# Chaining the first projections' low parts with the norms' statistics on VectorE, and the second chunk's statistics ahead of the first projection, in a two-layer transformer kernel

## The chip, the core and the metric

The kernel runs on one core of a Trainium2 chip. The metric is the device time of one execution in microseconds; 3 runs of the kernel before are shown. Five engines have instruction streams of their own: TensorE (PE; its weight loads are PEld), VectorE (DVE), ScalarE (ACT), GpSimd (POOL) and SyncE (SP), which only issues DMAs here. ScalarE issues DMAs as well, in line with its arithmetic: a DMA that has to wait for its data holds up what stands behind it on ScalarE.

## The reference

Two layers of the same weights, each with an attention block and a dense block, on x of 2048 rows and 512 columns:

```python
def _A_ref(x, wqkv, wo):                      # 32 heads of 16
    qkv = (x @ wqkv).reshape(B, S, 3, H, Dh).transpose(2, 0, 3, 1, 4)
    q, k, v = qkv[0], qkv[1], qkv[2]
    p = softmax(einsum("bhqd,bhkd->bhqk", q, k) * (Dh ** -0.5))
    o = einsum("bhqk,bhkd->bhqd", p, v)
    return o.transpose(0, 2, 1, 3).reshape(B, S, D) @ wo
def _B_ref(x, w1, b1, w2):                    # 512 -> 1792 -> 512
    h = x @ w1 + b1
    return (h * tanh(log1p(exp(-|h|)) + max(h, 0))) @ w2
for _ in range(2):
    x = x + _A_ref(layernorm(x), A_wqkv, A_wo)
    x = x + _B_ref(layernorm(x), B_w1, B_b1, B_w2)
```

## The kernel before

**Numbers.** Every large product is made of three matmuls of fp32r parts. A value is split into a high part (ScalarE copies it, rounded) and a low part (VectorE subtracts the high part from it), and the product is the sum of high by high, low by high and high by low: `mm3` (L159 to L164), and `mm3_by_kind` (L152 to L157) for the first two projections. `split_psum` (L148) is that split for a result that lies in PSUM, the matmuls' accumulator memory.

**Tiling.** The 2048 rows are cut into four chunks of 512. A chunk is normalised in four tiles of 128 rows and transposed, so that its columns can be multiplied by the weights. The projections to q, k are units (m, c): m is 0 to 3 for q's and 4 to 7 for k's blocks of 128 columns, c is the chunk; such a unit is 12 matmuls into one PSUM bank of the "s" kind, of which there are three. Units of v have four tiles of 12 matmuls each. The order of the units of layer 0 is a list written by hand: six of chunk 0, four of chunk 1, (3, 0), then (0, 2), (4, 2), (7, 0), (2, 1), (6, 1), (0, 3), (4, 3) and the others.

**Layer 0's start.** `first_norm` (L685) normalises chunk 0 at once, with warm-up matmuls in between. Chunks 1 to 3 are normalised by `norm_parts` (L166), a generator of five steps: first the statistics of the four tiles (L177 and L178 on VectorE, four pairs, chained with one another), the variance (L173) on VectorE and its power on GpSimd (L174); then four times a normalised tile (L196 on VectorE, name xnq), four transposes on TensorE (L201, bank tpq of the "n" kind, two of them), and the split (high thq L149 on ScalarE, low tlq L150 on VectorE). `steps` (L770) puts these steps ahead of given places in the list of units: chunk 1's five at 1 to 5 of the numbers it is given, chunk 2's from 6, chunk 3's from 11.

**After a unit**, `evict` (L455) splits its bank into pt (one of three buffers, shared with the raw weights that are being split in `make`, L111) and ScalarE issues the store scr<-pt (L458). When m 0 and m 4 of three chunks are stored, `prep_qk` (L230) issues on SyncE the loads of the first heads' rows of q and k (qs, ks; L249), then those of the last chunk. `some_max` (L446) puts pairs of score matmuls (pm, pn; L273) between the last units, whose maxima VectorE takes (L291, L306). A v tile is copied by ScalarE into one half of vst (L504) and stored by SyncE (L505).

**What sets the order.** The helper `Order` (L83) ties each instruction handed to it to the last one handed to it on the same engine: a fixed order with no semaphore. `front` is such a chain, used by `first_norm`, the statistics in `norm_parts`, and the first two units' matmuls. The attention has a chain of its own, in which all of its matmuls, reductions and exponentials stand. Whatever is in no chain is placed by a planner, which models the engines' times when the program is built and orders each engine's instructions by that model.

The lines that the change touches:

```python
def split_psum(hi, lo, src):
    nc.scalar.activation(hi, src, AF.Copy)
    nc.vector.tensor_tensor(lo, src, hi.bitcast(F32), op=ALU.subtract)
...
for c, at in ((1, range(1, 7)), (2, range(6, 12)), (3, range(11, 17))):
    steps(before, at, norm_parts(xc[c], f"q0{c}", tt, c, "n", o=front))
```

## Time and profile before

| | |
|---|---|
| median of 3 runs | 3481.96 us (3481.78 to 3482.94) |
| the profiled execution | 3478.88 us |
| its span, first to last instruction | 3476.9 us |
| TensorE busy | 3444.9 us, 99% of the span |
| VectorE busy | 2971.3 us, 85% |
| ScalarE busy | 2622.1 us, 75% |
| mean granted clock of TensorE | 0.996 of full speed |

The program has four stages in each layer: projections (0 to some 186 us in layer 0), attention, the output projection, and the dense block. Layer 1 begins near 1743 us. A busy share is a mean over stages that are bound by different engines, so the rows below are read stage by stage. Matmuls are pipelined: a row's duration is longer than its distance to the next one, and it is the distance that counts in a full stretch.

### The profile page before, as it was taken

To read this page: it belongs to the slowest core of one execution; us is meant where nothing else is said; L and a number is where in the kernel's file an instruction comes from. 1 tells how busy PE (TensorE), PEld (TensorE's weight loads), DVE (VectorE), ACT (ScalarE), POOL (GpSimd) and SP (SyncE) were. 2 spreads that over 40 slices of the span, in tenths; PEclk is the share of its full clock that TensorE was granted. 3 is DMA by queue.
4 is the path that set the end of the run, shared out by engine and by line. 5 is a ranking of instruction groups with operands and counts; after the bars stand their busy time and mean duration, and the time that the engine had idled before them with its cause. 6 is when DMAs were issued, how large, how long until landed. Compare 5 with 4: busy or idle time off the path is not lost.

```text
span 3476.9 us, 71195 instructions
## 1 busy us (share of the span) xinstructions
PE 3444.9 (99%) x29075; PEld 1919.7 (55%) x29075; DVE 2971.3 (85%) x4155; ACT 2622.1 (75%) x4893; POOL 282.1 (8%) x329
## 2 busy tenths in 40 slices
PE   9999999999999999999999999999999999999999
PEld 6644444444444444888876444444444444448887
DVE  6699999999999996665537999999999999956554
ACT  3188899899989887356532889998988998964665
POOL 1000000000000001222200000000000000012222
PEclk9999999999999999999999999999999999999999
DMA  7641312213122114500264202112021220154000
GB/s 257 223 108 34 81 43 74 61 54 80 45 58 55 31 55 122 180 13 13 86 200 154 53 15 46 35 27 49 20 48 20 42 43 18 56 144 157 13 13 25
DMA packets 131863, 247.39 MB, mean 71 GB/s; under 512 B 30928, under 2 KB 72400, under 8 KB 116432
## 3 DMA queue, kind: packets, MB, share of 16 engines
q1 hardware_dynamic: 110960, 186.21, 21.3%
q10 hardware_dynamic: 20576, 56.63, 4.2%
q8 instruction: 229, 3.75, 0.5%
q14 instruction: 98, 0.80, 0.1%
HBM read 149.43 MB, written 92.27 MB: 70 GB/s over the span
## 4 chain that ended last, share of the span: by engine, by line
DVE 66%; PE 29%; DMA 2%; issue 1%; ACT 1%; SPq 0%; DVEq 0%; ACTq 0%
DVE mxv L306 33%; DVE mxv L291 32%; PE h L164 3%; PE h L163 3%; PE h L162 3%; PE mo L162 3%; PE mo L163 3%; PE mo L164 3%; PE qk L162 1%; PE qk L163 1%; PE qk L164 1%; PE sp L353 1%; PE pv L379 1%; PE va L162 1%; PE wo L162 1%
## 5 line engine op out<-in xcount | busy, mean ns | idle before, releaser
L355 ACT ACTIVATE p<-sp 128x512 f32<-128x512 f32 x4096 | 2134.6, 598 | 239.6 <-PE pn L273 142.6
L291 DVE TENSOR_REDUCE mxv<-pm 128x2 f32<-128x1024 f32 x1024 | 1239.6, 1211 | 80.7 <-PE pm L273 80.7
L306 DVE TENSOR_REDUCE mxv<-pn 128x1 f32<-128x512 f32 x2048 | 1304.1, 675 | 2.8 <-PE pn L273 2.6
L353 PE MATMUL sp<-qs,ks 50*128 50x512 f32 x4096 | 1290.2, 447 | 0.2
L379 PE MATMUL pv<-p,va 128*32 128x256 f32 x16384 | 1196.7, 388 | 1.9 <-DVE pt L150 1.9
L353 PEld LDWEIGHTS sp<-qs,ks 50*128 50x128 f32 x4096 | 569.9, 184 | 712.1 <-ACT p L355 627.5
L273 PE MATMUL pn<-ks,qs 48*128 48x512 f32 x2048 | 824.0, 449 | 1.2 <-DVE mxv L306 0.9
L379 PEld LDWEIGHTS pv<-p,va 128*32 128x32 f32 x16384 | 377.6, 108 | 547.2 <-issue 428.9
L273 PE MATMUL pm<-ks,qs 48*128 48x512 f32 x2048 | 436.3, 421 | 1.0 <-DMA ks<-scr 1.0
L273 PEld LDWEIGHTS pn<-ks,qs 48*128 48x128 f32 x2048 | 365.6, 183 | 8.3 <-DVE mxv L306 2.7
L273 PEld LDWEIGHTS pm<-ks,qs 48*128 48x128 f32 x2048 | 193.1, 185 | 64.1 <-issue 8.0
L318 POOL CAST nh<-nm 128x16 fp32r<-128x16 f32 x64 | 12.7, 198 | 2437.4 <-DVE nm L313 2437.4
L633 POOL TENSOR_TENSOR hb<-hb,he 128x512 f32<-128x512 f32 x112 | 148.5, 1326 | 474.4 <-DVE he L630 474.4
L162 PE MATMUL mo<-w,ah 128*128 128x512 f32 x448 | 176.0, 394 | 3.4 <-ACT ah L636 3.3
L163 PE MATMUL mo<-w,ah 128*128 128x512 f32 x448 | 175.4, 392 | 0.0
L164 PE MATMUL h<-thm,w 128*128 128x512 f32 x448 | 175.0, 391 | 0.0
L163 PE MATMUL h<-tlm,w 128*128 128x512 f32 x448 | 174.9, 390 | 0.0
L162 PE MATMUL h<-thm,w 128*128 128x512 f32 x448 | 174.7, 391 | 0.0
L164 PE MATMUL mo<-w,al 128*128 128x512 f32 x448 | 166.8, 392 | 0.0
L635 DVE TENSOR_TENSOR hb<-hb,hr 128x512 f32<-128x512 f32 x112 | 77.3, 690 | 98.9 <-ACT hr L632 73.1
L627 ACT ACTIVATE hb<-h,b1t 128x512 f32<-128x512 f32 x112 | 76.9, 687 | 97.7 <-PE h L164 77.2
L149 ACT ACTIVATE pt<-qk 128x512 fp32r<-128x512 f32 x64 | 38.0, 598 | 146.8 <-PE qk L164 119.4
(130 smaller groups left out, 2555.0 us busy)
## 6 DMA issues: line engine op xcount, KB each, us to landing
scr<-pt ACTq DMA_DIRECT2D x64, 512.0 KB
ks<-scr SPq DMA_DIRECT2D x168, 128.0 KB
qs<-scr SPq DMA_DIRECT2D x168, 128.0 KB
vscr<-vst SPq DMA_DIRECT2D x32, 512.0 KB
va<-vscr SPq DMA_DIRECT2D x16, 1024.0 KB
w<-w1p SPq DMA_DIRECT2D x14, 1024.0 KB
w<-w2p SPq DMA_DIRECT2D x14, 1024.0 KB
raw<-ot SPq DMA_DIRECT2D x256, 32.0 KB
```

Of the source, the lines that this page charges most:

```text
L162: pe(nc.tensor.matmul(acc, ah, bh, start=first and i == 0, stop=False))
L163: pe(nc.tensor.matmul(acc, ah, bl, start=False, stop=False))
L164: pe(nc.tensor.matmul(acc, al, bh, start=False, stop=last and i == n - 1))
L273: nc.tensor.matmul(out, qs[h // 2][rows, q0 : q0 + P], ks[h // 2][rows, ts(c, 512)], start=True, stop=True)
L291: self.order(nc.vector.tensor_reduce(self.mxs[b][:, 0:2, qt, c], pm, axis=AX.X, op=ALU.max))
L306: self.order(nc.vector.tensor_reduce(self.mxs[b][:, h, qt, c : c + 1], pm, axis=AX.X, op=ALU.max))
L353: nc.tensor.matmul(sp, ks[h // 2][rows, ts(kt, P)], qs[h // 2][rows, ts(qb, CW)], start=True, stop=True)
L355: return lambda: self.order(nc.scalar.activation(self.pts[s][:, h], sp, AF.Exp, scale=SCALE))
L379: nc.tensor.matmul(acc[ts(h, VW), cols], va[:, kt, h, :], self.pts[s][:, h, cols], start=kt == 0 and half == 0, stop=kt == NKT - 1, skip_g ...
L627: nc.scalar.activation(hb, acc, AF.Identity, bias=b1t[:, f : f + 1])
L633: nc.gpsimd.tensor_tensor(hb, hb, e, op=ALU.mult)
L635: nc.vector.tensor_tensor(hb, hb, r, op=ALU.mult)
```

## The change

`split_psum` and `evict` get an argument o through which the low part's instruction on VectorE is passed. In layer 0 (where `first` is the chain `front`) the first 12 units in the list pass `front`, so their low parts stand in one chain with the statistics of chunks 1 to 3, in the order in which the program is written. The five steps of chunk 1's norm, at places 1 to 5 before, are at 0, 2, 3, 4 and 5: the statistics are ahead of the first unit.

```diff
--- before.py
+++ after.py
@@ -145,9 +145,9 @@
         nc.sync.dma_start(t.bitcast(F32), wparts[kind, j])
         return t
 
-    def split_psum(hi, lo, src):
+    def split_psum(hi, lo, src, o=lambda ins: ins):
         nc.scalar.activation(hi, src, AF.Copy)
-        nc.vector.tensor_tensor(lo, src, hi.bitcast(F32), op=ALU.subtract)
+        o(nc.vector.tensor_tensor(lo, src, hi.bitcast(F32), op=ALU.subtract))
 
     def mm3_by_kind(acc, pairs, pe=lambda ins: ins):
         n = len(pairs)
@@ -452,9 +452,9 @@
                 att.max_one()
                 att.max_one()
 
-        def evict(m, c, acc):
+        def evict(m, c, acc, o=lambda ins: ins):
             pt = tmp.tile([P, 2, CW], F32R, tag="raw", name=f"pt{l}{m}{c}", bufs=3)
-            split_psum(pt[:, 0], pt[:, 1], acc)
+            split_psum(pt[:, 0], pt[:, 1], acc, o)
             nc.scalar.dma_start(
                 scr[m][:, :, ts(c, CW)].bitcast(F32).rearrange("a p n -> p a n"), pt.bitcast(F32)
             )
@@ -516,7 +516,7 @@
                     pe=first if first and i < 2 else pe,
                 )
                 left -= 1
-                evict(m, c, acc)
+                evict(m, c, acc, first if first and i < 12 else lambda ins: ins)
                 if m in (0, 4):
                     done += 1
                     if done >= 2 * NCH - 2 and done % 2 == 0:
@@ -767,7 +767,7 @@
         at(i, lambda j=j: load_qkv(0, wts, (j,), later=wait, stores=stores, lo="dve"))
     for n in range(6):
         at(19 + n, lambda n=n: stores[n]())
-    for c, at in ((1, range(1, 7)), (2, range(6, 12)), (3, range(11, 17))):
+    for c, at in ((1, (0, 2, 3, 4, 5, 6)), (2, range(6, 12)), (3, range(11, 17))):
         steps(before, at, norm_parts(xc[c], f"q0{c}", tt, c, "n", o=front))
     for l in range(2):
         if l == 0:
```

The planner's order follows. Names: qk, then layer, chunk and m (qk020 is chunk 2, m 0); pt, then layer, m and chunk (pt002 is the same unit's split result); tpq, xnq: layer, chunk, tile; thq, tlq, stq, mvq: layer, chunk; vm: split weights of v; scr: the store's target, by layer and m. The number behind _ is a buffer's.

VectorE, around chunk 2's statistics, before:

```order
L150 TENSOR_TENSOR tlq01_272<-tpq012_331,thq01_271 128x4x128
L150 TENSOR_TENSOR tlq01_272<-tpq013_361,thq01_271 128x4x128
L178 BN_AGGR mvq03_529<-stq03_528 128x2
L177 BN_STATS stq03_528<-x03_103 128x6
L196 TENSOR_SCALAR xnq020_421<-x02_101,mvq02_389,rsq02_391 128x512
L196 TENSOR_SCALAR xnq021_450<-x02_101,mvq02_389,rsq02_391 128x512
L178 BN_AGGR mvq03_529<-stq03_528 128x2
L177 BN_STATS stq03_528<-x03_103 128x6
L150 TENSOR_TENSOR pt060_381<-qk006_368,pt060_381 128x512
L178 BN_AGGR mvq03_529<-stq03_528 128x2
L173 TENSOR_SCALAR veq03_530<-mvq03_529 128x4
L150 TENSOR_TENSOR pt001_415<-qk010_402,pt001_415 128x512
```

The two first normalised tiles of chunk 2 stand here ahead of pt060 and pt001, chunk 2's statistics are above this piece, and chunk 3's are spread over it. VectorE at the same place after:

```order
L150 TENSOR_TENSOR tlq01_272<-tpq012_331,thq01_271 128x4x128
L150 TENSOR_TENSOR tlq01_272<-tpq013_361,thq01_271 128x4x128
L150 TENSOR_TENSOR pt060_381<-qk006_368,pt060_381 128x512
L177 BN_STATS stq02_388<-x02_101 128x6
L178 BN_AGGR mvq02_389<-stq02_388 128x2
L177 BN_STATS stq02_388<-x02_101 128x6
L178 BN_AGGR mvq02_389<-stq02_388 128x2
L177 BN_STATS stq02_388<-x02_101 128x6
L178 BN_AGGR mvq02_389<-stq02_388 128x2
L177 BN_STATS stq02_388<-x02_101 128x6
L178 BN_AGGR mvq02_389<-stq02_388 128x2
L150 TENSOR_TENSOR pt001_415<-qk010_402,pt001_415 128x512
```

Chunk 2's four pairs now stand together between pt060 and pt001, and no statistics of chunk 3 are here.

TensorE, ahead of the first matmuls of chunk 2 (- before, + now):

```order
 L163 MATMUL qk003_511<-tlq00_111,qkm1_192 128x512
 L164 MATMUL qk003_511<-thq00_110,qkm1_192 128x512
+L201 MATMUL tpq022_478<-ident_70,xnq022_476 128x128 x4
+L201 MATMUL tpq023_504<-ident_70,xnq023_502 128x128 x4
 L162 MATMUL qk020_542<-thq02_419,qkm0_91 128x512
 L162 MATMUL qk024_570<-thq02_419,qkm2_95 128x512
-L201 MATMUL tpq030_563<-ident_70,xnq030_561 128x128 x4
+L162 MATMUL qk007_628<-thq00_110,qkm3_196 128x512
+L163 MATMUL qk007_628<-tlq00_111,qkm3_196 128x512
```

The last two tiles' transposes now stand directly ahead of chunk 2's first matmul, which is followed by qk007, a unit of chunk 0, instead of a transpose of chunk 3.

ScalarE at the same place, before:

```order
L149 ACTIVATE pt051_498<-qk015_485 128x512
L149 ACTIVATE thq02_419<-tpq022_478 128x4x128
L149 ACTIVATE thq02_419<-tpq023_504 128x4x128
L458 DMA scr05_205<-pt051_498 128x2x512
L149 ACTIVATE pt030_524<-qk003_511 128x512
L149 ACTIVATE thq03_559<-tpq030_563 128x4x128
L458 DMA scr03_203<-pt030_524 128x2x512
L149 ACTIVATE pt002_555<-qk020_542 128x512
```

Chunk 2's last two high parts (thq02) stand one behind the other here, ahead of two stores. ScalarE at the same place after:

```order
L149 ACTIVATE pt051_498<-qk015_485 128x512
L149 ACTIVATE thq02_419<-tpq020_423 128x4x128
L121 ACTIVATE vm1_355<-vr1_356 128x512 x2
L458 DMA scr05_205<-pt051_498 128x2x512
L149 ACTIVATE thq02_419<-tpq021_452 128x4x128
L149 ACTIVATE pt030_524<-qk003_511 128x512
L149 ACTIVATE thq02_419<-tpq022_478 128x4x128
L458 DMA scr03_203<-pt030_524 128x2x512
L149 ACTIVATE thq02_419<-tpq023_504 128x4x128
L149 ACTIVATE pt002_555<-qk020_542 128x512
L458 DMA scr00_200<-pt002_555 128x2x512
```

Now each of the last three has an eviction (pt051, pt030) or a store's issue (L458) ahead of it.

VectorE at the start of layer 1, where the last chunk's sums of layer 0's dense block (x203, L655) and its statistics (L584 to L586) meet the first low parts of layer 1, before:

```order
L655 TENSOR_TENSOR x203_18378<-mo03_20684,x203_18378 128x512 x2
L584 BN_STATS stq13_21363<-x203_18378 128x6
L585 BN_AGGR mvq13_21364<-stq13_21363 128x2
L584 BN_STATS stq13_21363<-x203_18378 128x6 x2
L585 BN_AGGR mvq13_21364<-stq13_21363 128x2
L586 TENSOR_SCALAR veq13_21365<-mvq13_21364 128x1
L585 BN_AGGR mvq13_21364<-stq13_21363 128x2 x2
L586 TENSOR_SCALAR veq13_21365<-mvq13_21364 128x1 x3
L597 TENSOR_SCALAR xnq130_21485<-x203_18378,mvq13_21364,rsq13_21366 128x512
L597 TENSOR_SCALAR xnq131_21504<-x203_18378,mvq13_21364,rsq13_21366 128x512
L150 TENSOR_TENSOR pt102_21384<-qk120_21371,pt102_21384 128x512
```

The first low part of layer 1, pt102, closes this piece. VectorE at the same place after:

```order
L584 BN_STATS stq13_21363<-x203_18378 128x6 x2
L655 TENSOR_TENSOR x203_18378<-mo03_20684,x203_18378 128x512 x2
L585 BN_AGGR mvq13_21364<-stq13_21363 128x2 x2
L584 BN_STATS stq13_21363<-x203_18378 128x6 x2
L586 TENSOR_SCALAR veq13_21365<-mvq13_21364 128x1 x2
L585 BN_AGGR mvq13_21364<-stq13_21363 128x2
L150 TENSOR_TENSOR pt102_21384<-qk120_21371,pt102_21384 128x512
L150 TENSOR_TENSOR pt140_21405<-qk104_21392,pt140_21405 128x512
```

The low parts pt102 and pt140 move ahead of the normalised tiles xnq130 and xnq131. On TensorE the last dense tile's 12 matmuls (mo, L162 to L164) stand behind 20 matmuls of the units qk120, qk104 and qk114 there, and ahead of them before.

Other places move by some rows: stores of weights (L128, on ScalarE) by up to 8 rows at 16 places of the attention, the loads of the last chunk's qs on SyncE.

## Rows read from the trace of the kernel before

**Rows 1.** The page's first part: busy time, share of span, instructions.

```profile
PE 3444.9 (99%) x29075; PEld 1919.7 (55%) x29075; DVE 2971.3 (85%) x4155; ACT 2622.1 (75%) x4893; POOL 282.1 (8%) x329
```

**Rows 2.** Busy time by stretch: window, length, PE, PEld, DVE, ACT, POOL, PEclk, DMA share, GB/s.

```profile
40.00:60.00 20.00, 20.00 (x103) 16.71 (x102) 11.55 (x20) 8.47 (x16) 0.00 (x0) 1.00 0.48 181
60.00:80.00 20.00, 18.98 (x83) 14.74 (x82) 6.42 (x9) 3.88 (x7) 0.00 (x0) 1.00 1.00 271
80.00:100.00 20.00, 19.31 (x86) 14.99 (x84) 4.06 (x6) 2.83 (x5) 0.00 (x0) 1.00 0.96 370
100.00:120.00 20.00, 19.12 (x78) 13.15 (x80) 11.21 (x15) 4.20 (x8) 0.00 (x0) 0.91 0.94 310
...
220.00:300.00 80.00, 80.00 (x818) 36.22 (x820) 79.93 (x108) 72.24 (x140) 7.62 (x8) 1.00 0.26 61
```

**Rows 3.** TensorE's timeline: start, duration, line, operation, tile, [idle before <- what ended it].

```profile
33.18 0.73 PE L162 MATMUL qk<-thq,qkm 128*128 128x512 f32 x2 [1.09 <-ACT thq L149]
34.85 0.50 PE L163 MATMUL qk<-tlq,qkm 128*128 128x512 f32 x1 [0.93 <-DVE tlq L150]
...
49.96 0.62 PE L162 MATMUL qk<-thq,qkm 128*128 128x512 f32 x2
...
65.54 0.61 PE L162 MATMUL qk<-thq,qkm 128*128 128x512 f32 x2
67.17 0.47 PE L273 MATMUL pm<-ks,qs 48*128 48x512 f32 x1 [1.02 <-DMA ks<-scr]
...
75.95 0.50 PE L162 MATMUL qk<-thq,qkm 128*128 128x512 f32 x1
...
100.88 0.50 PE L162 MATMUL va<-vm,thq 128*128 128x512 f32 x1 [1.57 <-ACT vst L504]
```

**Rows 4.** Chain of waits from 0 to 200 us: start, share of time, what.

```profile
57.72 4.35 DMA scr<-pt
...
63.82 3.32 DMA ks<-scr
...
71.78 5.08 DMA scr<-pt
...
89.81 6.01 DMA scr<-pt
...
97.01 3.12 DMA vscr<-vst
100.23 0.61 ACT vst L504
...
101.61 0.23 PE va L164
...
102.87 0.43 PE va L162
```

**Rows 5.** VectorE's timeline in layer 0's start.

```profile
15.07 0.68 DVE L177 BATCH_NORM_STATS2 stq<-x 128x6 f32<-128x512 f32 x1
...
15.89 0.66 DVE L177 BATCH_NORM_STATS2 stq<-x 128x6 f32<-128x512 f32 x1
...
23.81 1.00 DVE L196 TENSOR_SCALAR xnq<-x,mvq,rsq 128x512 f32<-128x512 f32 x2
...
35.38 0.98 DVE L196 TENSOR_SCALAR xnq<-x,mvq,rsq 128x512 f32<-128x512 f32 x2
...
36.95 0.67 DVE L150 TENSOR_TENSOR pt<-qk,pt 128x512 fp32r<-128x512 f32 x1
...
38.31 0.69 DVE L150 TENSOR_TENSOR pt<-qk,pt 128x512 fp32r<-128x512 f32 x1 [0.40 <-ACT pt L149]
```

**Rows 6.** GpSimd's timeline in layer 0's start.

```profile
19.54 1.02 POOL L174 TENSOR_TENSOR rsq<-veq,mhalf 128x4 f32<-128x4 f32 x1 [9.44 <-DVE veq L173]
```

**Rows 7.** VectorE's timeline at the start of layer 1.

```profile
1756.29 1.29 DVE L655 TENSOR_TENSOR x<-mo,x 128x512 f32<-128x512 f32 x2 [0.30 <-PE mo L164]
...
1763.72 1.29 DVE L150 TENSOR_TENSOR pt<-qk,pt 128x512 fp32r<-128x512 f32 x2 [0.54 <-ACT pt L149]
```

## The prediction

> **What bounds the kernel now.** I read the busy shares first, then the stretches of the first 300 us, then TensorE's own rows there, then VectorE's, then the chain of waits. TensorE is busy for 3444.9 of 3476.9 us [rows 1], so a change of order alone can win only the few us in which it waits or runs at half clock, and it can lose as much as it makes it wait anew. From 220 us on VectorE sets the pace: it is busy for 79.93 of 80 us [rows 2], in the attention, where the change adds nothing to it. So what counts is when the projections at the start of layer 0 and of layer 1 end. In layer 0's start TensorE is busy all of 40 to 60 us, and the DMA engines half of it (0.48); from 60 to 100 the DMA share is 1.00 and 0.96 [rows 2]. TensorE waits four times there: 1.09 and 0.93 us at chunk 1's first matmuls, 1.02 us for a load of ks at the first max pair [rows 3], and 1.57 us at a v matmul at 100.88 that waits for ScalarE's copy into vst, which waits for the store of an earlier vst [rows 3, 4]. At 49.96 and 65.54, the first matmuls of chunks 2 and 3, it does not wait [rows 3]. After 100.88 TensorE is full up to the attention, so a delay there is carried to the end.
>
> **The change part by part.** Nothing is added or removed in arithmetic; a low part keeps its 0.67 us and a pair of statistics its 0.82 us (0.68 at 15.07, the next at 15.89) [rows 5]. What changes is what stands ahead of what.
>
> Step 1, chunk 1. Its four pairs now stand ahead of all low parts of projections, so its first normalised tile can leave VectorE some 1.8 us earlier than 23.81 [rows 5]. But its first matmuls are paced by its last two high parts on ScalarE, which come behind a weight load, its split and an eviction. By the new order I walk ScalarE and VectorE row by row with the old durations and come to 34.5 for the matmul that is now at 34.85. Gain 0.35. Bounds: 0.93 gained (its whole wait [rows 3]) and 0.3 lost (half a low part ahead of the low part that it waits for).
>
> Step 2, chunk 2. Before, its statistics lay in VectorE's gaps, and its first two normalised tiles were made at 35.38, ahead of pt060 (36.95) and pt001 [rows 5]. Now four pairs stand in one row between these two: pt060's low ends at about 36.4, four pairs take 4 x 0.82 = 3.3, so pt001's low begins at 39.6 instead of 38.31. Behind it come the variance, GpSimd's power (1.02) [rows 6] and the tile itself: 39.6 + 0.7 + 0.2 + 1.0 = 41.5 instead of 35.38, six us late. Four tiles' transposes go down the PE order by one projection, and the last two stand directly ahead of chunk 2's first matmul. That was the situation of chunk 1, where the wait was 1.09 [rows 3]. Here the transposes also wait about 0.7 for a PSUM bank whose low part is behind the split of a weight, and the last high part stands on ScalarE behind pt030's store, whose issue waits for pt030's low part: some 1.35. New wait 0.7 + 1.35 = 2.05; bounds 1.1 (chunk 1's) and 3.0 (a second low part and its eviction, 2 x 0.67 with what lies between).
>
> Step 3, chunk 3. The same form: its last two transposes now stand directly ahead of its first matmul, and pt061's eviction (which needs a buffer whose store has just begun) ahead of the last high parts. No wait before; I take 1.2, near chunk 1's 1.09, bounds 0.9 and 2.4.
>
> Step 4, the first max pair goes 36 matmuls further down, so its 1.02 us wait [rows 3] goes, and two places where TensorE turned between max and projection matmuls become one (some 0.2 each: the pm row's 0.47 [rows 3] against 0.23 per matmul in the chain [rows 4]). Gain 1.4; bounds 1.0 and 1.4. At the row that is at 75.95 [rows 3] TensorE is then -0.35 + 2.05 + 1.2 - 1.4 = 1.5 us late.
>
> Step 5, the DMAs. This is larger than TensorE's own delay. The stores of chunk 2's first two projections are issued when their low parts are done. By the same walk the second goes from 57.72 [rows 4] to 62.2, the first is 3.9 later too. The chain of waits runs from that second store (4.35 us) through the loads of qs and ks (the last of the first lot at 63.82) to stores of 5.08 and 6.01 and the vst store that ends at 97.01 + 3.12 [rows 4]. So what now begins at 58 begins 3.6 to 4.4 us later. If other transfers fill the engines at the share of 0.48 meanwhile [rows 2], 0.52 x 3.6 = 1.9 of it remains at 100; if none does, 4.4. I take 3.5, since the chain shows the transfers end to end. The v matmul at 100.88 then begins at 104.4, and that contains steps 1 to 4: TensorE's 1.5 is in it and its wait there becomes 1.57 + 3.5 - 1.5 = 3.6. Behind it the clock falls to half (1.2 GHz): 0.43 instead of 0.23 us per matmul [rows 4]; by the mean of 0.91 over these 20 us [rows 2] that costs 1.8. The wait stays, so I keep it once.
>
> Beside this, a rule: the Trainium skill, "DMA: Bandwidth & Descriptors", section Anatomy of one DMA (it is told there for GpSimd's path), gives a transfer about 2.0 us plus its bytes over 436 GB/s; for a 524 kB store that is an estimate of 3.2 us. The rows have 4.35, 5.08 and 6.01 in this stretch, so here the rule is short by up to 2.8 and the queueing counts; by the rule the three would be 5.8 us shorter together, the store would be out of TensorE's way, and the result would be rival B.
>
> Step 6, layer 1. The planner's order moves there too: the last MLP tile's 12 matmuls stand behind 20 of the projections. From the sixth of the twelve on, when the first two sums are done, VectorE has ahead of the bank's release two additions (1.3), two statistics (2 x 0.68 [rows 5], 1.3 as they overlap), two additions (1.3) [rows 7], two aggregates (0.3), two statistics (1.3), small rows (0.3) and pt102's low part (0.7), which is now at 1763.72 [rows 7]: 6.5. TensorE has 6 + 11 + 5 = 22 matmuls x 0.23 = 5.1 until its fourth projection needs the bank that this low part reads. New wait 1.4. Bounds 0 (other order of arrival) and 2.4. Attention: stores and loads move by some rows, beside a full VectorE, at no cost; if that cover went, ScalarE's exponentials would be next, with 72.24 of 80 us [rows 2].
>
> Sum against the profiled execution (3478.88, 1.98 of it outside the span): 3.5 + 1.4 = +4.9, so 3483.8. The median shown is 3.08 above that execution; on it I predict 3481.96 + 4.9 = 3486.9. A measurement of this kernel can tell about 0.2%, 7.0 us, from no change, so this is "the same".
>
> **The rivals.** A is the forecast.
>
> B, absorbed. TensorE waits 1.57 at 100.88 for a DMA. If the engines catch up in the unused half of 40 to 60, that store ends when it did, TensorE's 1.5 us fall into the 1.57, and only step 6 stays: +1.4, 3483.4. For: a share of 0.48 just ahead. Against: 1.00 and 0.96 behind it [rows 2].
>
> C, gain: VectorE's row order is what the wait at chunk 1 came from, and chunks 2 and 3 find their high parts ready after all. Then 1.02 and 0.35 go, the wait of 1.57 goes because the loads come later than the stores of v, and the half clock behind it (1.8): -4.7, 3477.3. Against: six us later tiles for chunk 2 and no row that shows slack of six.
>
> D, slower: the v stores fall into the full stretch. Now the vst store takes 3.12 at 97.01, and the store just before 6.01 [rows 4]. vst has two halves, so each v tile's copy waits for the store two tiles before. If the full stretch lasts beyond 104 and two such stores take 6.01, that is 2 x 2.89 = 5.8 on top of 3.5 and 1.4: +10.7, 3492.7. It decides once one store takes over 5.2 (3.5 + 1.4 + 2.1 = 7.0). For: the loads start 4 us later and 0.94 is still the share at 100 to 120 [rows 2].
>
> E, the change doesn't do what it says: chunk 1's first matmul is paced by the weight load and is not earlier. That is within step 1, 0.35 at most, and changes no number above.
>
> **How the numbers follow.** A 0.55 (with E), B 0.20, C 0.09, D 0.16. A's own range is by its bounds 1.9 to 4.4 and 0 to 2.4: 3483.9 to 3488.8. For 8 in 10 I leave out most of C below and the upper half of D: 3478.0 to 3492.5. Faster by over 0.2% (below 3475.0) needs C and one more stretch at full clock: 0.04. Slower (above 3488.9): D and a tail of A, 0.18. Within: 0.78.
>
> **What would show it.** Right: first matmuls of chunks 2 and 3 with new waits of 1 to 3 us; no wait of the first max pair for ks; loads of qs beginning 3 to 4 us later; the v matmul of 100.88 at about 104; a wait of about one us in layer 1's fourth projection. Wrong: no wait at chunk 2 (steps 2 and 5 fall), that v matmul before 102.5 (B or C) or after 106 (D), a further stretch at half clock in 1 to 180 us, or a difference between 220 us and layer 1's start that isn't there at 220.

## The result, and the profile after

| | before | after |
|---|---|---|
| median | 3480.92 us (3477.65 to 3483.83, 13 runs) | 3488.76 us (3485.70 to 3491.18, 13 runs) |
| ratio | | 1.0023, 95% interval 1.0014 to 1.0031 |
| profiled execution, span | 3478.88, 3476.9 | 3487.59, 3485.8 |

The changed kernel is slower by 7.8 us, 0.23%, clear of the runs' scatter. That is past the 0.2% that the prediction took as its bound, though the interval (0.14 to 0.31%) spans it. It forecast +4.9 us and a range of 3478.0 to 3492.5; the direction and the range held, the size was short by 2.9. TensorE's busy time is that of before in sum (3444.9 us in both), but not stage by stage, as the next table and rows show.

TensorE's time at five marks that both kernels have, from their timelines (one profiled execution of each), shows where it was lost:

| mark | before | after | later by |
|---|---|---|---|
| first score matmul of layer 0's attention (L353) | 174.60 | 184.21 | 9.61 |
| first waiting matmul of its output projection (wo) | 1387.24 | 1397.53 | 10.29 |
| a late tile of the dense block (mo, its wait of 1.78) | 1749.59 | 1759.44 | 9.85 |
| first wait in layer 1's attention (pn) | 1903.95 | 1914.89 | 10.94 |
| layer 1's output projection (wo) | 3118.81 | 3126.24 | 7.43 |

All of it is there at 184 us. Layer 1's start adds 1.1, and layer 1's attention gives 3.5 back: before, TensorE's clock was at half (1.2 GHz) for 6.8 us right after 1904, and after it was not. Up to the first mark, before and then after:

```profile
0.00:174.60 174.60, 166.21 (x737) 120.50 (x737) 107.21 (x174) 44.10 (x76) 9.35 (x20) 0.99 0.71 239
```
```profile
0.00:184.21 184.21, 168.52 (x737) 122.08 (x737) 108.19 (x174) 43.80 (x76) 9.33 (x20) 0.97 0.67 227
```
With the same matmuls TensorE is busy 2.3 us longer, at a mean clock of 0.97 instead of 0.99, and idle 7.3 us longer (15.69 against 8.39). So of the 9.61 us three quarters are waiting and one quarter is half clock.

The stretches of after, with the columns of [rows 2]:

```profile
40.00:60.00 20.00, 17.41 (x76) 13.73 (x75) 14.13 (x30) 5.38 (x10) 2.02 (x2) 0.91 0.37 143
60.00:80.00 20.00, 19.21 (x93) 15.44 (x92) 7.36 (x12) 5.81 (x11) 0.00 (x0) 1.00 0.77 222
80.00:100.00 20.00, 19.93 (x88) 15.79 (x87) 5.69 (x8) 3.60 (x7) 0.00 (x0) 1.00 1.02 365
100.00:120.00 20.00, 13.99 (x53) 9.65 (x52) 5.68 (x7) 2.99 (x5) 0.00 (x0) 0.83 0.84 283
220.00:300.00 80.00, 80.00 (x823) 36.12 (x818) 79.93 (x107) 71.90 (x139) 5.82 (x8) 1.00 0.30 69
```
Against [rows 2] three things stand out. TensorE, full from 40 to 60 before, is busy 17.41 there, at a mean clock of 0.91. The DMA engines' share in that stretch fell from 0.48 to 0.37 and in the next from 1.00 to 0.77, so the full stretch begins later. And from 100 to 120 TensorE is busy for 13.99 instead of 19.12, with the clock at 0.83. The attention is as it was (79.93 of 80 on VectorE).

TensorE's timeline of after, as [rows 3]:

```profile
34.02 0.74 PE L162 MATMUL qk<-thq,qkm 128*128 128x512 f32 x2 [2.23 <-ACT thq L149]
34.86 0.51 PE L163 MATMUL qk<-tlq,qkm 128*128 128x512 f32 x1
...
51.54 0.63 PE L201 MATMUL tpq<-ident,xnq 128*128 128x128 f32 x4 [1.56 <-DVE tlq L150]
53.09 1.42 PE L162 MATMUL qk<-thq,qkm 128*128 128x512 f32 x3 [0.92 <-ACT thq L149]
54.30 0.63 PE L163 MATMUL qk<-tlq,qkm 128*128 128x512 f32 x1
...
57.07 0.39 PE L164 MATMUL qk<-thq,qkm 128*128 128x512 f32 x1
...
71.15 0.96 PE L162 MATMUL qk<-thq,qkm 128*128 128x512 f32 x3 [0.79 <-ACT thq L149]
...
79.52 0.50 PE L273 MATMUL pm<-ks,qs 48*128 48x512 f32 x2
...
109.65 0.79 PE L162 MATMUL va<-vm,thq 128*128 128x512 f32 x1 [6.01 <-ACT vst L504]
...
115.64 0.50 PE L162 MATMUL va<-vm,thq 128*128 128x512 f32 x1
```
The first matmul with a low part of chunk 1 is at 34.86, where it was at 34.85. Ahead of chunk 2's first matmul are waits of 1.56 and 0.92 us, and right behind it the clock is at half: the matmul at 54.30 has the duration 0.63, the one at 57.07 again 0.39. Chunk 3's first matmul waits 0.79 and comes at 71.15 instead of 65.54. The max pair at 79.52 has no wait for ks. The v matmul that waited 1.57 at 100.88 now waits 6.01 and comes at 109.65; the next v tile starts at 115.64, against 106.03 before, and from there all is 9.61 late.

The DMA engines between 55 and 65 us, before and then after:

```profile
55.00:65.00 10.00, 10.00 (x51) 8.25 (x50) 4.32 (x7) 3.26 (x6) 0.00 (x0) 1.00 0.79 232
```
```profile
55.00:65.00 10.00, 10.00 (x45) 8.21 (x45) 4.28 (x11) 2.41 (x5) 1.01 (x1) 0.91 0.14 52
```
0.79 against 0.14: before, this is where the loads of qs and ks begin, at 57.93; after, the engines have next to nothing to do until 64.74. ScalarE's timeline of after shows why (ACTq is a DMA's issue):

```profile
52.43 0.60 ACT L149 ACTIVATE thq<-tpq 128x512 fp32r<-128x512 f32 x1 [1.57 <-PE tpq L201]
60.69 0.60 ACT L149 ACTIVATE pt<-qk 128x512 fp32r<-128x512 f32 x1 [7.66 <-PE qk L164]
62.05 0.37 ACTq L458 DMA_DIRECT2D scr<-pt  x1
63.19 1.09 ACT L149 ACTIVATE pt<-qk 128x512 fp32r<-128x512 f32 x2 [1.90 <-PE qk L164]
...
64.80 1.42 ACTq L458 DMA_DIRECT2D scr<-pt  x2
```
Between the high part at 52.43 and the eviction at 60.69 no unit is finished. Three units, qk020, qk024 and qk007, are under way on TensorE in the three PSUM banks at once, at half clock for a part of it. The store of pt002 is issued at 62.05 and that of pt042 at 64.80, 7.1 us later than before both (54.95 and 57.72).

The chain of waits of after, as [rows 4]:

```profile
82.51 5.04 DMA scr<-pt
...
91.89 7.72 DMA qkp<-qkm
...
105.13 3.77 DMA vscr<-vst
109.00 0.61 ACT vst L504
```
The store of the last chunk is issued at 82.51, a store of split weights (qkp) takes 7.72 us in the full stretch, and SyncE comes to the vst store at 105.13, 8.1 us later than the 97.01 of before.

### The profile page after: what moved, and what is told of

Same layout as the page of the kernel before. It is cut to its first block, busy times and chain, and to the rows that moved or that the text cites. A ratio compares the mean times of both kernels' runs of the same rounds, so it can differ in the third digit from the quotient of the medians.

```text
span 3485.8 us, 71204 instructions
## 1 busy us (share of the span) xinstructions
PE 3444.9 (99%) x29075; PEld 1918.9 (55%) x29075; DVE 2971.6 (85%) x4155; ACT 2621.5 (75%) x4893; POOL 282.2 (8%) x329
## 3 DMA queue, kind: packets, MB, share of 16 engines
q8 instruction: 229, 3.75, 0.5%
## 4 chain that ended last, share of the span: by engine, by line
PE 55%; DVE 40%; DMA 3%; issue 1%; ACT 1%; SPq 1%; DVEq 0%; POOL 0%; ACTq 0%; POOLq 0%
DVE mxv L306 19%; DVE mxv L291 19%; PE pv L379 13%; PE sp L353 11%; PE pm L273 4%; PE h L163 3%; PE h L164 3%; PE h L162 3%; PE mo L162 3%; PE mo L163 3%; PE mo L164 3%; PE pn L273 2%; PE qk L162 1%; PE qk L163 1%; PE qk L164 1%; PE va L162 1%
## 5 line engine op out<-in xcount | busy, mean ns | idle before, releaser
L291 DVE TENSOR_REDUCE mxv<-pm 128x2 f32<-128x1024 f32 x1024 | 1255.1, 1226 | 82.6 <-PE pm L273 82.6
L306 DVE TENSOR_REDUCE mxv<-pn 128x1 f32<-128x512 f32 x2048 | 1318.8, 689 | 1.0 <-PE pn L273 0.9
L353 PE MATMUL sp<-qs,ks 50*128 50x512 f32 x4096 | 1290.2, 447 | 0.2
L353 PEld LDWEIGHTS sp<-qs,ks 50*128 50x128 f32 x4096 | 569.4, 184 | 711.6 <-ACT p L355 627.9
L162 PE MATMUL mo<-w,ah 128*128 128x512 f32 x448 | 175.5, 392 | 3.5 <-ACT ah L636 3.3
L164 PE MATMUL h<-thm,w 128*128 128x512 f32 x448 | 175.0, 391 | 0.0
L162 PE MATMUL h<-thm,w 128*128 128x512 f32 x448 | 174.7, 391 | 0.0
L164 PE MATMUL mo<-w,al 128*128 128x512 f32 x448 | 166.1, 390 | 0.0
```

The costliest lines, as they stand in the source:

```text
L162: pe(nc.tensor.matmul(acc, ah, bh, start=first and i == 0, stop=False))
L164: pe(nc.tensor.matmul(acc, al, bh, start=False, stop=last and i == n - 1))
L291: self.order(nc.vector.tensor_reduce(self.mxs[b][:, 0:2, qt, c], pm, axis=AX.X, op=ALU.max))
L306: self.order(nc.vector.tensor_reduce(self.mxs[b][:, h, qt, c : c + 1], pm, axis=AX.X, op=ALU.max))
L353: nc.tensor.matmul(sp, ks[h // 2][rows, ts(kt, P)], qs[h // 2][rows, ts(qb, CW)], start=True, stop=True)
```

## The experiments

Each kernel was measured beside the kernel before on the same chip. The theory from these rows: the chain holds chunk 2's and 3's statistics back, TensorE waits there, chunk 2's stores and with them the loads of qs and ks come later, and the vst store, which SyncE issues behind these loads, comes later by as much.

| kernel | ratio, 95% interval | in us | waits ahead of chunks 1, 2, 3 | DMA share 55 to 65 | vst store issued | vst waits | first score matmul |
|---|---|---|---|---|---|---|---|
| before | | | 2.0, 0, 0 | 0.79 | 97.01 | 1.6 | 174.6 |
| after | 1.0023 (1.0014 to 1.0031) | +7.8 | 2.2, 2.5, 0.8 | 0.14 | 105.13 | 6.0 | 184.2 |
| move_only | 1.0000 (0.9991 to 1.0009) | 0 | 1.6, 0, 0 | 0.86 | 95.62 | 0.6 | 171.7 |
| chain_only | 1.0041 (1.0028 to 1.0053) | +14 | 5.6, 0.8, 0.8 | 0.29 | 108.47 | 5.8 | 186.3 |
| chain_early | 1.0005 (0.9996 to 1.0014) | +2 | 1.8, 0.2, 0 | 0.65 | 98.70 | 1.5 | 174.5 |
| chain6 | 1.0028 (1.0017 to 1.0039) | +10 | 3.0, 2.0, 0.7 | 0.27 | 103.63 | 5.4 | 181.8 |
| early2 | 1.0016 (1.0008 to 1.0025) | +6 | 1.9, 0, 0.8 | 0.79 | 102.50 | 6.2 | 180.6 |
| early3 | 1.0035 (1.0023 to 1.0047) | +12 | 3.4, 2.1, 0.7 | 0.28 | 104.98 | 5.4 | 183.9 |
| pe_order | 1.0031 (1.0020 to 1.0043) | +11 | 3.3, 1.4, 1.2 | 0.21 | 106.46 | 6.3 | 184.9 |
| v_on_act | 1.0021 (1.0012 to 1.0030) | +7 | 3.2, 1.6, 0.8 | 0.21 | | 3.0 | 180.5 |
| late_after | 1.0012 (1.0003 to 1.0021) | +4 | 2.6, 2.7, 0.8 | 0.14 | 98.54 | 0 | 175.5 |
| move_v_act | 1.0004 (0.9995 to 1.0012) | +1 | 1.9, 0, 0 | 0.67 | | 0.7 | 173.6 |
| late_before | 1.0002 (0.9993 to 1.0011) | +1 | 2.0, 0, 0 | 0.67 | 91.33 | 0 | 173.3 |
| late_early | 1.0000 (0.9991 to 1.0009) | 0 | 2.1, 0.2, 0 | 0.72 | 90.39 | 0 | 172.2 |

The third column is the ratio's distance from 1 in us, rounded (for after, the difference of the medians). An interval is some 3 to 4 us to either side, so most of the kernels that are slower than before can't be told from one another by their times. The waits are TensorE's sums from its timeline in us, and all columns from the fourth on come from one profiled execution of each kernel; v_on_act and move_v_act issue the vst stores on ScalarE. In the four kernels chain_only, chain6, early3 and pe_order 5 to 7 runs stand behind the ratio, in the others 11 or 13.

**Which half of the change.** move_only makes only the move of chunk 1's steps, chain_only only the chain.

```diff
-    for c, at in ((1, range(1, 7)), (2, range(6, 12)), (3, range(11, 17))):
+    for c, at in ((1, (0, 2, 3, 4, 5, 6)), (2, range(6, 12)), (3, range(11, 17))):
```


> Only the places of chunk 1's five steps change (0, 2 to 5 instead of 1 to 5); no low part is chained. Theory (the loss comes from the chain, which holds chunk 2's statistics back until pt060's low part): no change, -2 to +2 us against before, no wait at chunk 2's first matmul, the v matmul that waits for ScalarE's vst copy still near 101 us. Rival 1 (the loss comes from putting chunk 1's statistics first): +5 to +9 us.

```diff
-    for c, at in ((1, (0, 2, 3, 4, 5, 6)), (2, range(6, 12)), (3, range(11, 17))):
+    for c, at in ((1, range(1, 7)), (2, range(6, 12)), (3, range(11, 17))):
```


> The low parts of the first 12 units are chained, chunk 1's steps stay at 1 to 5. Theory: +5 to +10 us as with the whole change, waits of 1.5 to 3 us together ahead of chunk 2's first matmul, the vst wait 4 to 7 us instead of 1.57. Rival 1: -2 to +3 us.

The move alone changes nothing that can be measured. The chain alone costs about 14 us (interval 10 to 18; the whole change 5 to 11). That is more than the 5 to 10 expected, and the wait is not where I expected it: 5.6 us at chunk 1 and 0.8 at chunk 2. TensorE's timeline of chain_only at chunk 1:

```profile
35.84 1.94 PE L201 MATMUL tpq<-ident,xnq 128*128 128x128 f32 x8 [4.79 <-DVE tlq L150]
38.59 1.65 PE L162 MATMUL qk<-thq,qkm 128*128 128x512 f32 x3 [0.81 <-ACT thq L149]
```
Without the move chunk 1's statistics stand in the chain behind pt000's low part, and the transposes wait 4.79 us for a bank whose low part is late. So rival 1 falls; by the trace the move, within the change, repairs a part of what the chain costs (2.2 us of wait at chunk 1 instead of 5.6).

**Undoing what the chain holds back.** The chain stays whole, only the places of chunk 2's and 3's statistics in it are earlier.

```diff
-    for c, at in ((1, (0, 2, 3, 4, 5, 6)), (2, range(6, 12)), (3, range(11, 17))):
+    for c, at in ((1, (0, 2, 3, 4, 5, 6)), (2, (3, 7, 8, 9, 10, 11)), (3, (8, 12, 13, 14, 15, 16))):
```


> The whole change, but chunk 2's statistics are written at place 3 and chunk 3's at place 8, so that the chain no longer holds them back. Theory: the loss goes, -3 to +2 us against before; no wait over 0.5 us at chunk 2's and chunk 3's first matmuls; the vst wait within 1.5 us of the 1.57 of before. Rival 2 (the loss is in the chain as such, or in what the planner moves later: the attention, layer 1): +4 to +9 us still.

+2 us with an interval that holds zero (-1.4 to +4.9 us). The waits, in TensorE's timeline of chain_early at chunk 2 and at the v tile:

```profile
50.36 0.73 PE L162 MATMUL qk<-thq,qkm 128*128 128x512 f32 x2 [0.22 <-ACT thq L149]
...
102.39 0.50 PE L162 MATMUL va<-vm,thq 128*128 128x512 f32 x1 [1.45 <-ACT vst L504]
```
0.22 and 1.45 us: no loss can be measured any more, with all twelve low parts still chained, and the first score matmul is where it was before (174.54, 174.60). So the chain as such costs nothing that these runs can tell, and rival 2's first half falls. Its second half, what the planner moved later in the program, is not tested by this kernel, because its layer 1 lacks the new waits of after. Two other things speak against it: after is 9.61 us late at 184 us already, and late_before (below) has the same new waits in layer 1 and is not measurably slower than before.

**Which chunk.** early2 puts only chunk 2's statistics early, early3 only chunk 3's.

```diff
-    for c, at in ((1, (0, 2, 3, 4, 5, 6)), (2, range(6, 12)), (3, range(11, 17))):
+    for c, at in ((1, (0, 2, 3, 4, 5, 6)), (2, (3, 7, 8, 9, 10, 11)), (3, range(11, 17))):
```


> The whole change, but chunk 2's statistics written at place 3; chunk 3's stay behind pt030's low part in the chain, and qk021 still stands between chunk 3's matmuls. Theory (two places add up, chunk 2's wait with its half clock, and chunk 3's late stores): no wait over 0.5 us and no half clock at chunk 2, chunk 3's first matmul at 66 to 68 us instead of 71.15, the vst wait 3 to 5 us, +2 to +5 us against before. Rival (chunk 2's lateness is the only cause): -1 to +2 us.

```diff
-    for c, at in ((1, (0, 2, 3, 4, 5, 6)), (2, range(6, 12)), (3, range(11, 17))):
+    for c, at in ((1, (0, 2, 3, 4, 5, 6)), (2, range(6, 12)), (3, (8, 12, 13, 14, 15, 16))):
```


> The whole change, but chunk 3's statistics written at place 8; chunk 2's stay between pt060 and pt001, and qk021 still stands between chunk 3's matmuls. Theory: waits at chunk 2 stay (2 to 3 us together), those at chunk 3 go (0.8), the vst wait stays at 5 to 6 us, +6 to +8.5 us against before. Rival (chunk 3's lateness is the main cause): +1 to +4 us.

early3 doesn't help, as the theory has it (+12, interval +8 to +16, instead of the 6 to 8.5 expected, with chunk 1's wait at 3.4, of which below; chunk 3's wait of 0.7 stays, which the theory had go). early2 takes chunk 2's wait away, but a larger part of the loss stays than I expected (+6 instead of 2 to 5, a vst wait of 6.2 instead of 3 to 5). TensorE's timeline of early2:

```profile
65.75 0.96 PE L162 MATMUL qk<-thq,qkm 128*128 128x512 f32 x3 [0.79 <-ACT thq L149]
...
106.22 0.79 PE L162 MATMUL va<-vm,thq 128*128 128x512 f32 x1 [6.21 <-ACT vst L504]
```
Chunk 3's first matmul is at 65.75, as before, and still the vst wait is 6.21; TensorE also waits 1.31 at 90.89 for a low part, which the table leaves out. So the two places don't add up: with chunk 2's statistics early, chunk 3's place alone makes the difference between a vst wait of 1.45 (chain_early) and one of 6.21. What SyncE stands behind there, its chain shows:

```profile
62.08 5.37 DMA scr<-pt
...
94.10 6.11 DMA qkp<-qkm
...
102.50 2.97 DMA vscr<-vst
```
The loads begin at 59.85, but SyncE issues none between 62.70 and 67.46, when the store issued at 62.08 has landed, and its last loads follow a store of split weights that lands at 100.21. The loads are also in another order there (the first three are of ks). How much of the wait each of them makes is not separated.

**Are the later low parts to blame?** chain6 chains the low parts of chunk 0's six units alone.

```diff
-                evict(m, c, acc, first if first and i < 12 else lambda ins: ins)
+                evict(m, c, acc, first if first and i < 6 else lambda ins: ins)
```


> The whole change, but only the first 6 units' low parts (those of chunk 0) are in the chain; the six of chunk 1, (3, 0) and (0, 2) are free. Chunk 2's statistics still stand behind pt060's low part. Theory (what costs is that chunk 2's statistics come after chunk 0's last low part): the waits ahead of chunk 2's first matmul stay (1.5 to 3.5 us together), the DMA engines are still near idle from 55 to 65 us, the vst wait is 4 us or more, +5 to +9 us against before. Rival (the later low parts hold up chunk 2's tiles and chunk 3's statistics): the wait at chunk 2 falls under 1 us, -1 to +3 us.

The waits at chunk 2 stay (2.0 together), the engines are little used from 55 to 65 (0.27), and TensorE's timeline has the vst wait:

```profile
107.64 0.80 PE L162 MATMUL va<-vm,thq 128*128 128x512 f32 x1 [5.41 <-ACT vst L504]
```
At +10 (interval 6 to 14) it is a little above the 5 to 9 expected. So chunk 2's statistics behind pt060's low part are enough; the six low parts behind them in the chain are not needed for the loss.

**How the lateness becomes 6 us at the vst store.** Three kernels. pe_order chains the matmuls so that chunk 3's two units are finished before qk021, which stands between their matmuls after the change.

```diff
-                    pe=first if first and i < 2 else pe,
+                    pe=first if first and (i < 2 or 16 <= i < 19) else pe,
```


> The whole change, and the matmuls of units (0, 3), (4, 3) and (1, 2) are chained on TensorE as written, so that chunk 3's two units are finished before the twelve matmuls of qk021, which stand between their first and their second matmuls with the whole change, and the low parts pt003 and pt043 come ahead of the first maximum on VectorE. Waits at chunks 1 and 2 are as with the whole change. Theory (the vst store waits on SyncE behind the last loads of qs and ks, and those for these two stores): the two stores 2 to 3.5 us earlier than with the whole change (78.9 and 82.5), the vst wait 6.0 falls to 3 to 4.5, projections end 2 to 4 us earlier, +4 to +6 us against before. Rival (the vst wait is set by full DMA engines alone): the wait stays at 5 us or more, +7 to +9 us.

VectorE's timeline of pe_order has the two low parts, pt003 and pt043, 2.4 and 2.8 us earlier than after the change (77.77, 81.23), and their stores are issued at 77.41 and 80.60, 1.5 and 1.9 us earlier:

```profile
75.33 0.69 DVE L150 TENSOR_TENSOR pt<-qk,pt 128x512 fp32r<-128x512 f32 x1 [3.54 <-ACT pt L149]
78.45 0.69 DVE L150 TENSOR_TENSOR pt<-qk,pt 128x512 fp32r<-128x512 f32 x1 [2.43 <-ACT pt L149]
```
and SyncE's has the vst store no earlier (start, issuing time, count):

```profile
106.46 17.61 SPq L505 DMA_DIRECT2D vscr<-vst  x8
```
The vst waits are 1.88 and 4.41. The time is +11, with chunk 1's wait an us longer than after the change. So that link of the theory fell: these two stores alone don't set the vst store. In this kernel's chain the last loads follow a store of split weights (qkp, 97.52) that took 8.04 us. v_on_act takes the vst store out of SyncE's row altogether.

```diff
-                    nc.sync.dma_start(
+                    (nc.scalar if l == 0 else nc.sync).dma_start(
                         vscr[:, :, c * NCH + t, :].rearrange("g p n -> p g n"),
```


> The whole change, and layer 0's stores of vst are issued by ScalarE behind the copy instead of by SyncE behind all loads of qs and ks. Theory (the vst store is late because it stands behind loads that are late): the vst wait falls from 6.0 us to under 2, its half clock with it, and +1 to +4 us remain against before, TensorE's own waits at chunks 2 and 3. Rival 3 (the 16 DMA engines are full, whoever issues): the wait stays at 4 us or more and the time at +6 to +9 us.

Between the two theories: TensorE's timeline of v_on_act has two waits, 3.0 us together, instead of one of 6.0.

```profile
100.77 0.50 PE L162 MATMUL va<-vm,thq 128*128 128x512 f32 x1 [0.72 <-ACT vst L504]
...
106.69 0.50 PE L162 MATMUL va<-vm,thq 128*128 128x512 f32 x1 [2.24 <-ACT vst L504]
```
The first score matmul comes 3.7 us earlier than after the change; whether the measured time does (+7, interval 4 to 10) these runs can't tell. Half of the wait went with SyncE's row. For the rest the chain of v_on_act has the store that TensorE waits for:

```profile
99.71 6.25 DMA vscr<-vst
```
Issued at 99.71, it took 6.25 us where after the change it took 3.77. late_after takes traffic away instead. Six stores of split weights, which are needed in layer 1 alone, run among the loads of qs and ks; here they are issued behind the v tiles.

```diff
-        at(19 + n, lambda n=n: stores[n]())
+        at(27 + n, lambda n=n: stores[n]())
```


> The whole change, and the six stores of split weights (qkp, vp, issued by ScalarE from 85 us on, between the loads of qs and ks) are issued behind the v tiles, at places 27 to 32 instead of 19 to 24. TensorE's waits at chunks 1 to 3 stay. Theory (the late chunks move the whole full stretch of the DMA engines back by some 8 us, and the vst store waits for what is in that stretch): with four of these stores out of it the vst wait falls from 6.0 to under 2.5 us, projections end 3.5 to 7 us earlier than with the whole change, +1 to +4.5 us against before. Rival (SyncE's order alone, the loads wait for stores whoever else uses the engines): the wait stays at 4 us or more, +6 to +9 us.

The stretches of late_after (columns as [rows 2]) and SyncE's first vst store:

```profile
80.00:100.00 20.00, 20.00 (x89) 16.13 (x88) 5.69 (x8) 3.79 (x7) 0.00 (x0) 1.00 0.81 240
100.00:120.00 20.00, 20.00 (x91) 13.94 (x90) 12.02 (x15) 4.19 (x7) 0.00 (x0) 1.00 0.74 222
```
```profile
98.54 23.33 SPq L505 DMA_DIRECT2D vscr<-vst  x10
```
The vst wait is gone: TensorE is busy 20.00 of 20 us from 100 to 120, and the DMA share from 80 to 100 is 0.81. Chunks 1 to 3 wait as after the change (2.6, 2.7, 0.8), the engines are as idle at 55 to 65 (0.14), and yet projections end 8.7 us earlier than after the change, more than the 3.5 to 7 expected. So the vst wait comes from these stores, and what the late chunks did was to push the full stretch back by 8 us. The diff takes these stores off the DMA engines and also out of ScalarE's row, where they stand among the stores of pt; no run separates the two. The Trainium skill, "DMA: Bandwidth & Descriptors", section "Issuing engines are not separate DMA queues", says that DMAs of every issuing engine run on the same 16 engines and interleave. late_after agrees: stores that ScalarE issues, taken away, end a wait of 6.0 us for a store that SyncE issues. In v_on_act another issuer took off 3.0 of the 6.0; there that store no longer stands behind SyncE's loads.

**Is there a better kernel?** The kernel before has a wait of 1.57 us at the same place, so I tried to take it away there.

> The kernel before with only chunk 1's steps at 0 and 2 to 5, no chain, and layer 0's vst stores issued by ScalarE. Theory (the 1.57 us wait of before comes from SyncE's order): the vst wait under 0.5 us and no half clock at 100 to 106 us, projections end 2 to 4 us earlier than before, -1 to -4 us. Rival (ScalarE's issues hold up its evictions instead, or the engines are full): 0 to +3 us.

move_v_act is move_only's diff and v_on_act's, on the kernel before; late_before and late_early are late_after's diff on the kernel before and on chain_early.

> The kernel before, with the same six stores at places 27 to 32. Theory: the 1.57 us wait and the half clock behind it go, projections end 2 to 4 us earlier, -4 to 0 us against before. Rival (those stores then meet the attention's first loads, and TensorE or VectorE waits there): 0 to +4 us.

> The whole change with chunk 2's and 3's statistics written at places 3 and 8, and the six stores at 27 to 32. Theory: as late_before, no vst wait, -4 to +1 us against before. Rival (the chain itself costs some us): +2 to +6 us.

In all three the wait is gone or halved, the projections end 1.0 to 2.4 us earlier, at the low end of the 2 to 4 expected or below it, and none is faster: the intervals hold 1. move_v_act's wait (0.72) is no shorter than move_only's (0.58), so another issuer did nothing there; less traffic took the wait away. And the rival written for late_before shows in the traces of all three kernels with late stores: new waits at the attention's start, here in late_after,

```profile
178.54 0.50 PE L353 MATMUL sp<-qs,ks 50*128 50x512 f32 x1 [1.76 <-DVE pt L150]
```
and 1.76 and 1.60 in late_before and late_early, where the kernel before waits 0.46. Nothing here beats the kernel before.

## Why the prediction was right, step by step

- **Step 1 (chunk 1, gain 0.35): no gain.** 34.86 against 34.85. That was E, the case that the weight load sets the pace. ScalarE's timeline, before and then after:

```profile
27.78 0.63 ACT L121 ACTIVATE vm<-vr 128x512 fp32r<-128x512 f32 x1 [0.85 <-DMA vr<-in_A_wqkv_dram]
```
```profile
28.61 1.15 ACT L121 ACTIVATE vm<-vr 128x512 fp32r<-128x512 f32 x2 [1.38 <-DMA vr<-in_A_wqkv_dram]
```
Chunk 1's first matmul comes 5.40 us behind this split before (33.18) and 5.41 after (34.02). In the eight other kernels that have the order of before, of move_only or of after up to there, it is 5.39 to 5.54, while the split itself begins between 27.48 and 29.89. move_only and move_v_act have the same order there, and it begins at 27.48 and 29.09. So the first waits of 2.6 to 3.4 us in late_after, chain6, v_on_act, pe_order and early3 follow the landing of this load; whether the change delays it by some tenths these runs don't tell.
- **Step 2 (chunk 2, 2.05): right in mechanism and nearly in size.** 1.56 for the bank and 0.92 for the high part, 2.48. What the step left out is the clock: behind these waits it was at half, as [rows 4] show it behind the wait at 100.88 (chain6 has waits of 1.07 and 0.94 there and a granted clock of 1.00 from 40 to 60, so it need not be). The rows from 53.09 to 56.44 have a distance of 0.43 instead of 0.23, and over nine matmuls that is 1.7 (3.75 us instead of 9 x 0.23). The prediction named "a further stretch at half clock" as a sign of being wrong, and gave it no price.
- **Step 3 (1.2): 0.79**, below its bound of 0.9. **Step 4:** the 1.02 us wait went, as said.
- **Step 5 (the DMAs, 3.5): right in mechanism, short in size, and the step that makes the difference.** The v matmul came 8.8 us later. Two terms were mis-sized. The stores of pt002 and pt042 went back by 7.1 us, not 3.9 and 4.5: 3.2 more at pt002, of which 1.4 is chunk 2's first matmul (53.09, by the walk 49.96 - 0.35 + 2.05 = 51.66) and 1.7 the half clock. And 3.5 was taken below the whole delay, between its own cases that other work fills the engines meanwhile (1.9) and that none does (4.4): the share in the gap was 0.14, not 0.48, so nothing was given back, and the full stretch moved as a whole. The loads begin 6.8 us later, the vst store 8.1. A bound that took the whole delay of the stores, 7.1, would have come near it.
- **Half clock behind the vst wait: "once" was right, its length was not.** The mean clock from 100 to 120 is 0.83 instead of 0.91; by the prediction's reckoning that is 3.4 us lost instead of 1.8. The rows give less, since a part of that stretch is the wait itself: the same 16 matmuls from the waiting one to the next tile take 5.99 us instead of 5.15, 0.84 more.
- **Step 6 (layer 1, 1.4): right in place, near in sum, and in part by luck.** TensorE's timeline at layer 1's start:

```profile
1759.44 0.50 PE L162 MATMUL mo<-w,ah 128*128 128x512 f32 x1 [1.78 <-ACT ah L636]
...
1763.59 0.73 PE L162 MATMUL qk<-thq,qk 128*128 128x512 f32 x2 [0.69 <-ACT thq L149]
...
1775.41 0.50 PE L162 MATMUL qk<-thq,qk 128*128 128x512 f32 x1 [0.65 <-DVE pt L150]
...
1794.61 0.50 PE L163 MATMUL qk<-tlq,qk 128*128 128x512 f32 x1 [0.41 <-DVE tlq L603]
```
The fourth projection waits 0.65 for VectorE's low part (1775.41), less than half of the 1.4, and two others of 0.69 and 0.41 come with it, 1.75 together. Between the marks before and behind it the time grew by 1.1 only, because TensorE's busy time there fell by 0.66: before, the clock was at half from 1750.6 on, behind the wait at 1749.59 (mean 0.84 up to 1760), and after the change it was at 1.00 in the same place. The prediction had neither.
- **Attention at no cost: right** (79.93 of 80 in both).
- **The rivals.** B and C are out. D forecast +10.7 us (3492.7), which is as far above the measured +7.8 as A's +4.9 is below it, but from a mechanism that wasn't there: it needed vst stores of 6 us each, and the chain has 3.77 at 105.13 against 3.12 before. It began late, it didn't take long. (In v_on_act, where it was issued at 99.71, it did: 6.25.)
- **The signs.** As said came the wait at chunk 2 and the first max pair without a wait for ks. Not as said: chunk 3's wait is under 1 us, the loads begin 6.8 us later instead of 3 to 4, and the v matmul is at 109.65 instead of 104. Two of its signs of being wrong came too: a v matmul after 106, which it had put down to D, and a further stretch at half clock.

So the path was right (late statistics, late stores, late loads, a longer vst wait), its main term was too small, and that the measured time lies within the range is partly luck. A's own bounds add up to +1.9 to +6.8; the range held +7.8 because it had room for D. And the profiled execution lost 9.6 to 10.9 us up to layer 1's attention, and 3.5 of it came back there by a half-clock stretch that was not taken, which nothing in the forecast foresaw.

## What to carry to other kernels

Before chaining instructions on one engine in program order, see whether the statements are written in the order in which their results are needed: here the same chain cost 8 us with chunk 2's and chunk 3's statistics at places 6 and 11, and nothing that could be measured with them at places 3 and 8. Moving chunk 2's alone (+6) or chunk 3's alone (+12) was not enough. When a step delays stores that feed loads, look at what the DMA engines do meanwhile: here they were idle in the gap (0.14) and full behind it (1.02), and the whole delay moved through the full stretch and appeared at the vst store, its last transfer that TensorE waited for. Stores that nobody needs soon are worth trying elsewhere: without them that wait went, though in the kernel before the time didn't fall.

## What the runs showed of the hardware that I had not expected

**Where one half-clock stretch was missing, there was another one later.** The stretches 100 to 120 and 180 to 220 us of move_only, and 180 to 220 of the kernel before:

```profile
100.00:120.00 20.00, 20.00 (x91) 13.92 (x90) 13.25 (x17) 4.18 (x7) 0.00 (x0) 1.00 0.95 313
180.00:220.00 40.00, 39.44 (x361) 17.24 (x363) 35.45 (x47) 31.80 (x61) 0.42 (x2) 0.88 0.33 78
```
```profile
180.00:220.00 40.00, 39.06 (x392) 17.97 (x392) 39.28 (x52) 34.89 (x68) 0.42 (x2) 1.00 0.39 88
```
move_only has the clock at 1.00 from 100 to 120, where the kernel before has 0.91 [rows 2] behind its wait of 1.57, and 0.88 from 180 to 220, where the kernel before has 1.00; TensorE has no wait from 100 us up to the attention there. In move_only the half clock begins at 175.7, right behind the attention's first wait of 0.46 us, at 174.71; the kernel before has the same wait at 177.63, and its clock stays at 1.00. It holds in the profiled executions of all six kernels without a half-clock stretch at 100 to 120 (0.88 to 0.96 in the later one) and in seven of the eight with one (1.00; chain_only has 0.96). From the first score matmul to the output projection's wait it is 1212.6 us before, 1217.9 in move_only, 1216.7 in late_after. So of 8.7 us that late_after won at the projections' end 3.4 were lost there (1.3 of them by more waiting, 2.1 by longer busy time), and the gains of move_only and late_before (2.9 and 1.3) are no gains in the end. Why the clock falls in the later stretch is not settled by these runs; that the one stretch comes because the other is missing is not shown.

**Transfers in the full stretch took far longer than one alone would by the rule.** The qkp store of 1.05 MB took 7.72 us at a share near 1. By the rule of the Trainium skill's page "DMA: Bandwidth & Descriptors", section Anatomy of one DMA (about 2.0 us plus the bytes over 436 GB/s, told there for GpSimd's path; this store is ScalarE's), an estimate would be 4.4.
